# Seven products for the last down pair of groups 0 and 1, in a linear-attention block mixed with a gated feed-forward

## The chip, the cores and the metric

The kernel runs on one core of one Trainium2 chip. The metric is the device time of one execution in microseconds; the time before is the median of three runs.

## What is computed

```python
B, S, D = 1, 2048, 640;  F = 1536;  H = 32; Dh = 20
g = sigmoid((x * gate_w).sum(-1, keepdims=True))
# a: linear attention
q, k, v = split heads of x @ wqkv
phi = lambda t: where(t > 0, t + 1, exp(t)) + 1e-6
pq, pk = phi(q), phi(k)
kv = einsum("bhsd,bhse->bhde", pk, v);  z = pk summed over s
o = einsum("bhqd,bhde->bhqe", pq, kv) / (einsum("bhqd,bhd->bhq", pq, z) + 1e-6)
a = o @ wo
# b: gated feed-forward
b = (sigmoid(x @ w_gate) * (x @ w_up)) @ w_down
out = g * a + (1 - g) * b          # all float32
```

## The kernel before

**Layout.** Everything is transposed: rows of 128 features on the partitions, tokens along the free axis. The 2048 tokens are four groups of 512 (`TG`), D is 5 chunks of 128 (`KC`), F is 12 blocks of 128 (`FC`). A float32 product is three matmuls in a reduced format: each operand is split in a high half (a ScalarE copy that rounds) and a low half (a VectorE subtraction), and `mm3` (lines 406 to 408) multiplies high by high, high by low, low by high. Below, a "product" is one `mm3` of 128 x 128 weights by 128 x 512 values, and a "form" is an operand with its two halves.

**Seven products for eight.** Where two groups and two chunks make a 2 x 2 by 2 x 2 block product, the kernel uses the seven products of Winograd's form of Strassen's method, on sums of the operands (S1 to S4 of the weights, T1 to T4 of the values). Partial results are shared by seeding a PSUM bank with another bank's contents (a ScalarE copy) and adding further products to it.

**Stages.** The keys' side comes first and yields a 640 x 640 matrix M. Then `f_phase` runs the feed-forward for two groups at a time: groups 2 and 3 first (`pr` = 1), then groups 0 and 1 (`pr` = 0). For each of the 12 f blocks, `Block.s1` to `s7` compute gate and up for both groups; gate ends in the tiles c11 (group 0) and c12 (group 1), which become h. After every two f blocks `down_pair` multiplies h by that pair's rows of `w_down` and adds the ten results (5 chunks o, 2 groups g) to the tile `tb`. It is a generator: `f_phase` runs its four parts between steps 3, 4, 5 and 7 of the odd f block that follows. Inside it `new` starts a product in a fresh bank, `go` adds one to a bank, `seed` copies a bank, `out` adds a bank to `tb` on VectorE. B11, B21 are h of the pair's two f blocks for the first group, B12, B22 for the second; T1 = B11 - B12, T2 = B22 - T1, T4 = B21 - T2, T3 = B22 - B12.

The last pair (f blocks 10 and 11) has no following f block. `tail_f` makes plain forms of its h, and `last_down` computes its ten results in two products each (`down_term`, `down_unit`), 20 products. For `pr` = 0 three of the ten banks are seeded with `tb` and copied back by ScalarE, the others are added to `tb` on VectorE.

Last comes the attention part: p (phi of q, kept in DRAM as `p_dram`) is loaded, scaled by factors (`pq_scale`, VectorE), split into `pq`, and multiplied by M: first groups 2 and 3 by `a_unit` (each five terms of `mm3`, one for each chunk of M), then groups 0 and 1 by `ABlock`, which adds its results to `tb`.

**The order of the work.** The instruction order of every engine is written out when the kernel is built. The class `Order` keeps model clocks for TensorE, ScalarE and VectorE. Work that isn't tied to a place is queued with its costs; `order.fill()` puts in what ends no later than the model's TensorE clock plus a slack (`slack_a`, `slack_v`; `order.slack(False)` is 0.6 and 1.2 us). The queues have ranks: `items`, `lazy`, `chain`, `spare`; `streams` are taken by due time, some 2 us ahead (`EARLY`) at the latest. `order.need(key)` emits all that is queued under the key there and then. DMAs are issued by SyncE (`sp`) and GpSimd (`gp`), each in program order.

Of the kernel before, what the change touches and what calls it, by code (L numbers as in the profile page):

```python
# [373 lines left out]
def gated_mix_kernel(ctx: ExitStack, tc: tile.TileContext, xt, xn, wk, wv, wo, wst_q, wst_f, out_t):  # L374
# [1285 lines left out]
    def queue_m(u=0):  # L1660

        raw = down_pool[1].tile([P, D], F32, name="mr", tag="mr")
        m_rows(raw, None, sp, u)

        def fn():
            t = down_pool[1].tile([P, 2, D], F32R, name="mt", tag="mt")
            split(t[:, 0], t[:, 1], raw)

            def rest():
                gp.dma_start(mp_dram[:, u], f32(t))  # L1670
                if u + 1 < KC:
                    queue_m(u + 1)
            order.then(rest)
        order.add(a_cost(D), v_cost(D), fn, "m", lambda: order.when(raw) + 2, spare=True)

    def m_close():
# [106 lines left out]
    def tail_s(f, blk):  # L1783
# [37 lines left out]
    seen = set()  # L1821

    def down_pair(pr, p):
# [4 lines left out]
        def weights(form, q):  # L1828
            c = at[form] + 2 * q * P if form in at else (2 * D - P, D - P)[form == "w1"]
            if not pr:  # L1830
                h, l = (wf[0][:, i] for i in range(2))
            elif c < 2 * D:
                (h, l), c = WD["f", 1, 2 * p + 1 - c // D], c % D
            else:
                (h, l), c = DS[p], c - 2 * D
            return h[:, c:c + P], l[:, c:c + P]
# [21 lines left out]

        if pr:
            for j in range(2):  # L1860
                order.need(("d", ("f", 1, 2 * p + j)))
# [54 lines left out]

    def down_unit(pr, f, o, g, ps=None, seeded=False):
# [6 lines left out]
        if seeded:  # L1924
            act(dst, ps, AF.Copy, "p")
        else:
            add(dst, ps, dst, "p")

# [79 lines left out]
    def f_phase(pr, q, hooks={}):  # L2008
# [7 lines left out]
        for f, s in [(0, 1), (0, 2)] + [e for f in range(FC) for e in f_steps(f)]:  # L2016
            order.plan[pr, f, s] = at
            at += mm * n_mm[s]
        order.plan[pr, FC + 1, "d0"] = at - EARLY

        def step(f, s):
# [24 lines left out]
            if s == 7:  # L2046
                tails[f] = tail_f(f, blk, f == FC - 2) if f >= FC - 2 else tail_s(f, blk)
            if f + 2 < FC and not pr:
# [27 lines left out]
        for f in range(FC):  # L2076
# [53 lines left out]
    def last_down(pr, units):  # L2130
# [3 lines left out]
        order.slack_a, order.slack_v = 0.6, 0.8  # L2134
        if pr:
            omg = f32(down_pool[1].tile([P, 2, 8 * P], F32R, name="ds", tag="ds"))[:, :, :TG]
# [7 lines left out]

        seeds = {} if pr else {5: "cc", 7: "ch", 9: "cc"}

        def seed(i):
            if i in seeds:
                g, o = divmod(i, KC)
                early[i] = ps_tile(seeds[i])  # L2150
                act(early[i], tb[:, o, g], AF.Copy)
        for i in units[:4]:
            g, o = divmod(i, KC)
            if i not in seeds:
                early[i] = ps_tile("rot" if (o + g) % 2 else "dd")
            down_term(early[i], pr, FC - 2, o, g, i not in seeds)
        for i in units:
            g, o = divmod(i, KC)
            if i in seeds and i > 3:
                down_term(early[i], pr, FC - 2, o, g, False)  # L2160
            down_unit(pr, FC - 2, o, g, early.pop(i, None), i in seeds)
            seed(i + 4)
            if pr:
                order.add(0, v_cost(TG), lambda i=i: scaled(i), ("tb", i),
                          lambda: order.vec + 0.6, lazy=True)
            order.fill()
# [74 lines left out]
    def load_p(g):  # L2241

        n = groups.index(g)
        if n == 0:
            PL[g] = [tt("pl") for _ in range(KC - 1)]
            PL[g].append(f32(wu_tile()).rearrange("p a b -> p (a b)")[:, :TG])
            for u in range(KC):
                sp.dma_start(PL[g][u], p_dram[:, u, g])
        else:
            PL[g], PL[g, "t"] = [], []  # L2250
            for u in range(0, KC, 2):
                t = (x2_tile if n == 1 else h_tile)(dt=F32)
                w = min(2, KC - u)
                sp.dma_start(t[:, :w], p_dram[:, u:u + w, g])
                PL[g] += [t[:, i] for i in range(w)]
                PL[g, "t"].append(t)
        PL[g, "at"] = lambda: max(order.when(t) for t in PL[g])

    def load_b(g):
# [3 lines left out]
        elif g == groups[0]:  # L2263
            BL[g] = [ct("bl") for _ in range(KC)]
            for o in reversed(range(KC)):
                sp.dma_start(BL[g][o], b_dram[:, o, g - 2])
# [36 lines left out]
    def queue_pq(g):  # L2303
        for u in range(KC):
            order.add(a_cost(TG), v_cost(TG), lambda u=u: split(*PQ[g][u], PL[g][u]), ("pq", g, u))

# [51 lines left out]
    def queue_pt():  # L2358
# [22 lines left out]
        return queue  # L2381

    def a_first():
# [222 lines left out]
```

## Time and profile before

| | |
|---|---|
| runs | 730.27, 730.38, 730.37 us; median 730.37 |
| profiled execution | span 728.6 us from the first to the last instruction; the page gives no other time for it, and the median is 1.77 us above the span |
| TensorE (PE) | busy 724.0 us (99%), 3569 matmuls |
| VectorE (DVE) | busy 564.0 us (77%) |
| ScalarE (ACT) | busy 360.1 us (49%) |
| GpSimd (POOL) | busy 97.0 us (13%) |
| DMA | 173.54 MB, mean 238 GB/s |
| granted TensorE clock | 1.000 |

In the rows that follow, a line such as `L423 DVE TENSOR_TENSOR tb<-dd,tb` names the source line (423, a helper), the engine, the operation and the tiles, output first; `x3` is the number of instructions merged into the row. Times are microseconds from the start of the span unless they are the nanoseconds of one instruction. The busy time of TensorE counts overlapping matmuls once; the spacing of their starts is what one costs.

### The profile page before, as it was taken

Reading aid. Unit: us, or ns where it says so; the run is one execution under the profiler, and the core shown is the slowest. Engines: PE = TensorE matmul, PEld = TensorE weight load, DVE = VectorE, ACT = ScalarE, POOL = GpSimd, SP = SyncE. Lnnn points to the kernel's source line nnn. Section 1 sums busy time; section 2 is a strip of 40 time slices with the busy share of each in tenths; the row PEclk is TensorE's granted clock in tenths of the full one; section 3 lists DMA queues with packets and bytes.
Section 4 is the critical chain, followed back from the end, with each engine's and each line's share of the span. In section 5 each row is a group of like instructions: output and inputs, shape, how many; then the busy total and the mean of one; then the engine's idle time right before and its main releaser. Section 6 shows DMA issues by size and latency. Waiting matters only on the chain.

```text
span 728.6 us, 10106 instructions
## 1 busy us (share of the span) xinstructions
PE 724.0 (99%) x3569; PEld 622.6 (85%) x3569; DVE 564.0 (77%) x989; ACT 360.1 (49%) x668; POOL 97.0 (13%) x161
## 2 busy tenths in 40 slices
PE   9999999999999999999999999999999999999997
PEld 8999999988888888888888888888888888888886
DVE  6899778987687889888999973547685867698783
ACT  6884649357657653545355363354332332334550
POOL 0211111113212211211110031001000041000000
PEclk9999999999999999999999999999999999999999
DMA  8565658698787866557687288879889697869212
GB/s 269 148 181 111 183 129 253 146 343 292 266 315 260 331 220 232 199 223 252 260 327 261 98 300 321 304 233 339 266 285 325 219 330 210 292 221 337 85 61 102
DMA packets 72841, 173.54 MB, mean 238 GB/s; under 512 B 11690, under 2 KB 35258, under 8 KB 69206
## 3 DMA queue, kind: packets, MB, share of 16 engines
q1 hardware_dynamic: 55526, 109.99, 46.4%
q0 software_dynamic: 17120, 62.74, 24.4%
q8 instruction: 28, 0.46, 0.2%
q14 instruction: 23, 0.19, 0.1%
q10 hardware_dynamic: 144, 0.16, 0.1%
HBM read 103.96 MB, written 63.92 MB: 230 GB/s over the span
## 4 chain that ended last, share of the span: by engine, by line
PE 99%; DVE 0%; issue 0%
PE ch L406 11%; PE ch L407 11%; PE ch L408 11%; PE cc L407 9%; PE cc L408 9%; PE cc L406 9%; PE dd L407 8%; PE dd L408 8%; PE dd L406 8%; PE rot L407 6%; PE rot L408 6%; PE rot L406 6%; PE rot L1505 1%; PE rot L494 0%; PE ch L980 0%; PE dd L980 0%
## 5 line engine op out<-in xcount | busy, mean ns | idle before, releaser
L419 ACT ACTIVATE c<-ch 128x512 f32<-128x512 f32 x52 | 31.1, 598 | 94.9 <-PE ch L408 94.9
L423 DVE TENSOR_TENSOR hf<-c,hf 128x512 fp32r<-128x512 f32 x75 | 51.1, 687 | 24.7 <-ACT hf L419 24.4
L419 ACT ACTIVATE hf<-c 128x512 fp32r<-128x512 f32 x75 | 46.0, 625 | 27.3 <-DVE c L423 27.2
L423 DVE TENSOR_TENSOR c<-cc,c 128x512 f32<-128x512 f32 x40 | 27.6, 690 | 37.5 <-PE cc L408 23.8
L406 PE MATMUL ch<-xth,ws 128*128 128x512 f32 x112 | 43.7, 390 | 0.0
L408 PE MATMUL ch<-xth,ws 128*128 128x512 f32 x112 | 43.6, 389 | 0.0
L407 PE MATMUL ch<-xtl,ws 128*128 128x512 f32 x112 | 43.6, 389 | 0.0
L423 DVE TENSOR_TENSOR tb<-rot,tb 128x512 f32<-128x512 f32 (+1 forms) x61 | 39.3, 674 | 3.0 <-PE rot L408 3.0
L423 DVE TENSOR_TENSOR tb<-dd,tb 128x512 f32<-128x512 f32 x44 | 30.2, 686 | 8.7 <-PE dd L408 8.7
L406 PE MATMUL dd<-xrh,wg 128*128 128x512 f32 x90 | 35.2, 391 | 0.0
L408 PE MATMUL dd<-xrh,wg 128*128 128x512 f32 x90 | 35.1, 389 | 0.0
L407 PE MATMUL dd<-xrl,wg 128*128 128x512 f32 x90 | 35.0, 389 | 0.0
L419 ACT ACTIVATE c<-dd 128x512 f32<-128x512 f32 x22 | 13.1, 597 | 43.6 <-PE dd L408 43.6
L423 DVE TENSOR_TENSOR c<-c,c 128x512 f32<-128x512 f32 x46 | 31.6, 687 | 2.6 <-ACT c L419 2.0
L406 PE MATMUL cc<-xbh,ws 128*128 128x512 f32 x84 | 32.7, 389 | 0.0
L407 PE MATMUL cc<-xbl,ws 128*128 128x512 f32 x84 | 32.7, 389 | 0.0
L408 PE MATMUL cc<-xbh,ws 128*128 128x512 f32 x84 | 32.7, 389 | 0.0
L419 ACT ACTIVATE dd<-ch 128x512 f32<-128x512 f32 x22 | 12.8, 582 | 33.6 <-PE ch L408 33.6
L423 DVE TENSOR_TENSOR wst<-wst 128x256 f32<-128x256 f32 (+2 forms) x69 | 27.4, 413 | 1.4
L408 PEld LDWEIGHTS ch<-xth,ws 128*128 128x128 f32 x112 | 21.0, 188 | 4.7 <-DVE ws L423 0.3
L407 PEld LDWEIGHTS ch<-xtl,ws 128*128 128x128 f32 x112 | 21.0, 188 | 4.3
L406 PEld LDWEIGHTS ch<-xth,ws 128*128 128x128 f32 x112 | 21.0, 188 | 4.2
(643 smaller groups left out, 2354.1 us busy)
## 6 DMA issues: line engine op xcount, KB each, us to landing
wf<-ws POOLq DMA_DIRECT2D x12, 1152.0 KB, 7.5
ws<-wf SPq DMA_DIRECT2D x11, 1152.0 KB, 8.2
wst<-wst_f SPq DMA_DIRECT2D x12, 640.0 KB, 5.0
wf<-wg POOLq DMA_DIRECT2D x12, 640.0 KB, 6.5
wd<-wd POOLq DMA_DIRECT2D x12, 640.0 KB, 7.9
wg<-wf SPq DMA_DIRECT2D x12, 640.0 KB, 5.5
wf<-wd SPq DMA_DIRECT2D x10, 640.0 KB, 9.4
xnst<-xn SPq DMA_DIRECT2D x16, 320.0 KB, 3.7
```

What stands on the lines that cost most here:

```text
L406: nc.tensor.matmul(out, l_hi, r_hi, start=first, stop=False, skip_group_check=True)
L407: nc.tensor.matmul(out, l_hi, r_lo, start=False, stop=False, skip_group_check=True)
L408: nc.tensor.matmul(out, l_lo, r_hi, start=False, stop=last, skip_group_check=True)
L419: nc.scalar.activation(out, src, fn, **kw)
L423: nc.vector.tensor_tensor(out, a, b, op=op)
L1505: nc.tensor.matmul(ps[:w, :w], v[:, m, :w], gt[:, m, c0:c0 + w], start=(m == 0), stop=(m == KC - 1))
```

## The change

For groups 0 and 1 the last pair (f blocks 10 and 11) also runs through `down_pair`, in a branch of its own with another order of the products; `last_down` is left to groups 2 and 3. `tail_last` makes its forms. The sums of the weights for that pair are computed by a new chain of spare work (`queue_last_s`, behind the five steps of `queue_m`), stored, and loaded again by `load_last_s`. Four results (`FAR`) are copied out of PSUM by ScalarE and added to `tb` by a transfer that accumulates (`far`), two in the pair of blocks 8 and 9 and two in the last one. The first group's p is loaded in three steps (`load_p0`), its scalings are queued with each load, and its splits are queued after step 5 of block 11 instead of after step 7. `load_ms(1)`, and the scalings and splits of the second group, are queued behind the last pair; group 2's b results are loaded from the first to the last.

```diff
@@ queue_m: after the last of its five steps
+                else:
+                    queue_last_s()
@@
+    def queue_last_s():
+        p, w = FC // 2 - 1, 4 * P
+        raw = [down_pool[1].tile([P, D], F32, name=n, tag=n)[:, :w] for n in ("mr", "mv")]
+        for j in range(2):
+            sp.dma_start(raw[j], wst_f[2 * p + j, :, 2, :w])
...
+        def sums(part):
+            if part == 0:
+                add(a22, a21, a22)
+                sub(a21, a11, a21)
+            else:
+                sub(a11, a22, a11)
+                sub(a12, a12, a11)
+        def form(j):
+            t = down_pool[1].tile([P, 2, D], F32R, name="mt", tag="mt")[:, :, :w]
+            split(t[:, 0], t[:, 1], raw[j])
...
+                gp.dma_start(dst, f32(t))
...
@@ 
+    def tail_last(f, blk):
+        p = f // 2
+        def t3():
+            HR[p, "B21"] = blk.c11
+            h_form(p, "B21")
+        def t4():
+            act(blk.c12, blk.c12, AF.Sigmoid)
+            vec2(blk.c12, blk.c22, blk.c12, OP.mult, "a")
+        def t5():
+            HR[p, "B22"] = HR[p, "T3"] = b22 = blk.c12
+            HR[p, "T2"], HR[p, "T4"], b12 = t2, t4, _ = [HR.pop((p, n)) for n in ("T1", "B21", "B12")]
+            order.need(("h", p, "T1"), False)
+            sub(t2, b22, t2)
+            sub(t4, t4, t2)
+            h_form(p, "B22")
+            h_form(p, "T2")
+            sub(b22, b22, b12)
+        return {3: t3, 4: t4, 5: t5}
...
+    FAR = [(FC // 2 - 2, 1, 0), (FC // 2 - 2, 3, 0), (FC // 2 - 1, 4, 0), (FC // 2 - 1, 0, 0)]
@@ down_pair
+        def far(key, o, g):
+            if not far_at:
+                far_at.extend(down_pool[1].tile([P, D], F32, name="far", tag=n) for n in ("mr", "mv"))
+            t = far_at.pop(0)[:, :TG]
+            act(t, ps[key], AF.Copy, "p")
+            gp.dma_start(tb[:, o, g], t, accum_op=OP.add)
+            order.fill()
...
+            if not pr and (p, o, g) in FAR:
+                far(key, o, g)
+                return
...
+        if p == FC // 2 - 1:
+            new("W", "dd", "w0", "B11")
+            new("X0", "ch", "A11", "B11")
+            seed("V", "dd", "W")
+            new("X1", "ch", "A11", "B11", 1)
+            seed("Y0", "rot", "X0")
+            seed("Y1", "rot", "X1")
+            yield
+            new("Z0", "cc", "S1", "T1")
+            out("Z0", 1, 1)
+            new("Z1", "cc", "S1", "T1", 1)
+            out("Z1", 3, 1)
+            go("V", "w1", "B21")
+            out("V", 4, 0)
+            go("Y0", "A12", "B21")
+            out("Y0", 0, 0)
+            go("Y1", "A12", "B21", q=1)
+            out("Y1", 2, 0)
+            go("W", "w0", "T1")
+            go("X0", "S2", "T2")
+            out("X0", 0, 1)
+            go("X1", "S2", "T2", q=1)
+            out("X1", 2, 1)
+            go("Z0", "S4", "B22")
+            out("Z0", 0, 1)
+            go("Z1", "S4", "B22", q=1)
+            out("Z1", 2, 1)
+            go("X0", "S3", "T3")
+            out("X0", 1, 1)
+            go("X1", "S3", "T3", q=1)
+            out("X1", 3, 1)
+            go("W", "w1", "B22")
+            out("W", 4, 1)
+            go("X0", "A22", "T4")
+            out("X0", 1, 0)
+            go("X1", "A22", "T4", q=1)
+            out("X1", 3, 0)
+            return
@@ f_phase
-        order.plan[pr, FC + 1, "d0"] = at - EARLY
+        if pr:
+            order.plan[pr, FC + 1, "d0"] = at - EARLY
+        else:
+            for s, n in (("d1", 1), (3, 8), ("d2", 13), ("d3", 15)):
+                order.plan[pr, FC + 1, s] = at + mm * n
...
-                    load_ms(1)
...
             else:
+                if not pr:
+                    queue_t1(f // 2)
                 step(f, 6)
...
+            elif not pr:
+                tail_last(f, blocks[f])[3]()
+                order.slack_a, order.slack_v = 0.3, 0.3
             step(f, 7)
@@ 
+    def load_p0(u0, u1):
+        g = groups[0]
+        t = PL.setdefault(g, [])
+        for u in range(u0, u1):
+            t.append(tt("pl") if u < KC - 1 else f32(wu_tile()).rearrange("p a b -> p (a b)")[:, :TG])
+            sp.dma_start(t[u], p_dram[:, u, g])
+            order.add(0, v_cost(TG), lambda u=u: pq_scale(g, u), ("sc", g), lambda u=u: order.when(t[u]) + 1, lazy=True)
...
+    def load_last_s():
+        p = FC // 2 - 1
+        DS[p] = [x2_tile("ds", F32R).rearrange("p a b -> p (a b)") for _ in range(2)]
+        for c in range(2):
+            sp.dma_start(f32(DS[p][c]), wd_dram[p][:, c, 2 * D:])
     tail = f_phase(0, q, {
         (2, 7): [queue_m],
         (FC - 2, 2): [lambda: load_wd(FC - 2)],
-        (FC - 2, 7): [lambda: load_p(groups[0]), lambda: queue_scale(groups[0], True)],
-        (FC - 1, 2): [lambda: load_wd(FC - 1)],
+        (FC - 3, 4): [lambda: load_p0(0, 2)],
+        (FC - 2, 3): [lambda: load_p0(2, 4)],
+        (FC - 2, 7): [lambda: load_p0(4, 5)],
+        (FC - 1, 2): [lambda: load_wd(FC - 1), load_last_s],
+        (FC - 1, 5): [a_first],
         (FC - 1, 7): [lambda: load_m(1)],
     })
-    for s in (3, 4, 5):
-        tail[s]()
-    a_first()
+    down = down_pair(0, FC // 2 - 1)
+    order.slack_a = order.slack_v = -9.0
+    tail[4]()
+    next(down)
+    tail[5]()
+    order.slack_a, order.slack_v = 0.6, 0.8
+    for name in ("T3", "T4"):
+        queue_h(FC // 2 - 1, name)
     load_p(groups[1])
-    pq_tiles(groups[1])
     for g in groups[:2]:
         load_b(g)
+    for _ in down:
+        pass
+    order.slack(False)
+    load_ms(1)
+    pq_tiles(groups[1])
     queue_scale(groups[1])
     queue_pq(groups[1])
-    last_down(0, range(2 * KC))
```

More of the change, by code (lines that the diff above doesn't have):

```diff
@@ L1672, in rest @@
                     queue_m(u + 1)
+                else:
+                    queue_last_s()
             order.then(rest)
         order.add(a_cost(D), v_cost(D), fn, "m", lambda: order.when(raw) + 2, spare=True)
+    def queue_last_s():
[3 more added lines that the diff above has]
+            sp.dma_start(raw[j], wst_f[2 * p + j, :, 2, :w])
+        (a11, a21), (a12, a22) = [r.rearrange("p (q h c) -> h p q c", q=2, h=2) for r in raw]
+        at = lambda: max(order.when(r) for r in raw) + 1
+        ready = [at]
+        def sums(part):
[8 more added lines that the diff above has]
+            split(t[:, 0], t[:, 1], raw[j])
+            dst = wd_dram[p][:, :, 2 * D + j * w:2 * D + (j + 1) * w]
+            ready[0] = lambda: 1e9
+            def rest():
+                gp.dma_start(dst, f32(t))
+                ready[0] = lambda: order.when(dst)
+            order.then(rest)
+        for part in range(2):
+            order.add(0, 2 * v_cost(2 * P), lambda part=part: sums(part), "m", at, spare=True)
+        for j in range(2):
+            order.add(a_cost(w), v_cost(w), lambda j=j: form(j), "m", lambda: ready[0](), spare=True)
     def m_close():
@@ L1915, in down_term, with down_unit @@
         mm3(ps, h[:, os_], l[:, os_], *HT[f, g], first, not first)
[L1917 removed]
+    def down_unit(pr, f, o, g, ps=None):
         if ps is None:
@@ L1923, in down_unit @@
         dst = tb[:, o, g]
[L1924 to L1927, printed above, removed]
+        add(dst, ps, dst, "p")
     def q_phase(pr, b12, extra):
@@ L2046, in step @@
             if s == 7:
-                tails[f] = tail_f(f, blk, f == FC - 2) if f >= FC - 2 else tail_s(f, blk)
+                tails[f] = tail_f(f, blk, f == FC - 2) if pr and f >= FC - 2 else tail_s(f, blk) if f < FC - 1 else tail_last(f, blk)
             if f + 2 < FC and not pr:
@@ L2143, in scaled @@
             gp.dma_start(b_dram[:, o, g], tb[:, o, g])
[L2145 to L2151, printed above, removed]
         for i in units[:4]:
             g, o = divmod(i, KC)
-            if i not in seeds:
-                early[i] = ps_tile("rot" if (o + g) % 2 else "dd")
-            down_term(early[i], pr, FC - 2, o, g, i not in seeds)
+            early[i] = ps_tile("rot" if (o + g) % 2 else "dd")
+            down_term(early[i], pr, FC - 2, o, g, True)
         for i in units:
             g, o = divmod(i, KC)
[L2159 to L2165, printed above, removed]
+            down_unit(pr, FC - 2, o, g, early.pop(i, None))
+            order.add(0, v_cost(TG), lambda i=i: scaled(i), ("tb", i),
+                      lambda: order.vec + 0.6, lazy=True)
             order.fill()
@@ L2241, in load_p @@
     def load_p(g):
[L2243 to L2256, printed above, removed]
+        PL[g], PL[g, "t"] = [], []
+        for u in range(0, KC, 2):
+            t = (x2_tile if g == groups[1] else h_tile)(dt=F32)
+            w = min(2, KC - u)
+            sp.dma_start(t[:, :w], p_dram[:, u:u + w, g])
+            PL[g] += [t[:, i] for i in range(w)]
+            PL[g, "t"].append(t)
         PL[g, "at"] = lambda: max(order.when(t) for t in PL[g])
@@ L2264, in load_b @@
             BL[g] = [ct("bl") for _ in range(KC)]
-            for o in reversed(range(KC)):
+            for o in range(KC):
                 sp.dma_start(BL[g][o], b_dram[:, o, g - 2])
@@ L2304, in queue_pq @@
         for u in range(KC):
-            order.add(a_cost(TG), v_cost(TG), lambda u=u: split(*PQ[g][u], PL[g][u]), ("pq", g, u))
+            order.add(a_cost(TG), v_cost(TG), lambda u=u: split(*PQ[g][u], PL[g][u]), ("pq", g, u), lambda: PL[g, "at"]())
     def scale_b(g, o):
@@ L2381, in queue_pt @@
         return queue
+    def load_p0(u0, u1):
[5 more added lines that the diff above has]
+            order.add(0, v_cost(TG), lambda u=u: pq_scale(g, u), ("sc", g), lambda u=u: order.when(t[u]) + 1, lazy=True)
+        PL[g, "at"] = lambda: max(order.when(t) for t in PL[g])
     def a_first():
```

8 lines of the change are left out of this document (4 added, 4 removed).

## The prediction

> **What bounds the kernel now.** I read the page first, then the busy time by windows for the stage that changes, then the timelines of TensorE, VectorE and ScalarE there. The first two lines below are the page's busy time, the next its chain of work that ended last.
>
> ```profile
> span 728.6 us, 10106 instructions
> PE 724.0 (99%) x3569; PEld 622.6 (85%) x3569; DVE 564.0 (77%) x989; ACT 360.1 (49%) x668; POOL 97.0 (13%) x161
> PE 99%; DVE 0%; issue 0%
> ```
>
> TensorE is the bound, and its own order of matmuls is the chain: nothing else ends last anywhere. So a matmul that goes is worth its full spacing, and every wait that the change puts ahead of a matmul is paid in full. The stage that changes, by windows (columns: PE, PEld, DVE, ACT, POOL, each busy us and instructions, then clock, DMA share, GB/s) and by the timeline of TensorE (start, us, engine, ...):
>
> ```profile
> 645.65:659.25 13.60, 13.60 (x62) 11.27 (x60) 11.62 (x19) 6.62 (x12) 0.00 (x0) 1.00 0.99 374
> 634.77:645.65 10.88, 10.88 (x50) 9.01 (x48) 10.18 (x18) 1.75 (x3) 0.00 (x0) 1.00 0.12 31
> 645.42 0.39 PE L408 MATMUL cc<-xbh,ws 128*128 128x512 f32 x1
> 645.65 0.39 PE L406 MATMUL dd<-hf,wg 128*128 128x512 f32 x1
> 659.02 0.39 PE L408 MATMUL cc<-hf,wg 128*128 128x512 f32 x1
> 659.25 0.39 PE L406 MATMUL rot<-pq,ws 128*128 128x512 f32 x1
> ```
>
> The second window is the end of f block 11 (second half of step 5 to step 7), the first is `last_down`: 60 weight loads, so 60 matmuls, in 13.60 us, 0.2267 us each, 0.680 us for a product of three. The clock is granted in full. From 659.25 the attention part runs (`a_unit`). VectorE is busy 10.18 of 10.88 us in the second window while TensorE never waits: it is almost full, and can become the bound.
>
> **The change: products.** `last_down` has 2 blocks x 5 outputs x 2 groups = 20 products. The new branch of `down_pair` has 5 `new` and 13 `go`, 18 products. Removed: 2 x 3 matmuls x 0.2267 = 1.36 us. All of it is on the path, since PE is 99% of the chain. By the Trainium skill (TensorE: Matmul & The Clock Gate, Back-to-back issue gap) a 512-column matmul that is warm follows the last after N / 2.4 + 2.5 ns, 216 ns, which would make it 1.29 us. I take the row.
>
> **The chain behind step 7.** The old order ran four independent products first; the new one needs sums of the last block's result. What the chain costs, from the rows of before (the step's last matmul is the 645.42 row above):
>
> ```profile
> 645.85 0.69 DVE L423 TENSOR_TENSOR c<-cc,c 128x512 f32<-128x512 f32 x1
> 646.57 0.63 ACT L419 ACTIVATE c<-c 128x512 f32<-128x512 f32 x1 [3.62 <-DVE c L423]
> 647.24 0.69 DVE L423 TENSOR_TENSOR c<-c,c 128x512 f32<-128x512 f32 x1
> 648.03 0.63 ACT L419 ACTIVATE hf<-c 128x512 fp32r<-128x512 f32 x1 [0.82 <-DVE c L423]
> 615.71 1.41 DVE L423 TENSOR_TENSOR c<-c,c 128x512 f32<-128x512 f32 x2
> 653.25 1.89 DVE L423 TENSOR_TENSOR pq<-pl,pq 128x512 fp32r<-128x512 f32 x3
> 649.60 1.66 ACT L419 ACTIVATE pq<-pl 128x512 fp32r<-128x512 f32 x3
> ```
>
> A VectorE pass is 0.69 us, one that waits for the pass before it starts 0.72 after it (1.41 for two), independent ones follow every 0.60 (1.89 for three); ScalarE's copies follow every 0.52. A result can be read 0.43 us after its last matmul starts, 0.88 after its product starts. Let t = 0 be the start of the first down product behind step 7 (645.65 in the old trace).
>
> - Add 0.20, sigmoid 0.92, product with c22 1.59, T2 = B22 - T1 at 2.31, T4 = B21 - T2 at 3.03 (both wait for the one before).
> - ScalarE after the sigmoid: three PSUM seeds (V, Y0, Y1; 1.44, 1.96, 2.48), then the high halves of B22 (3.00) and T2 (3.52).
> - VectorE: low half of B22 3.66, of T2 4.26 (done 4.95), T3 4.86.
> - TensorE meanwhile: W, X0, X1 on B11 from 0; Z0, Z1 on T1 from 2.04; V, Y0, Y1 on B21 from 3.40; W on T1 5.44; X0 and X1 on T2 from 6.12. So T2 is a microsecond early; no wait.
>
> **Results added on VectorE.** 14 results are taken out of PSUM in the last pair; two of them (V, Y0) go by ScalarE and a transfer, 12 stay on VectorE. From 5.46, every 0.60: Z0 5.46, Z1 6.06, Y1 6.66, low half of T3 7.26 (the planner starts it some 2 us ahead of its due time, 13 products), X0 7.86, X1 8.46, low half of T4 9.06, Z0 9.66, Z1 10.26, X0 (output 1, group 1) 10.86, done 11.55. The seventeenth product, X0 on T4, adds to the same PSUM bank, which must have been read; without a wait it would start at 16 x 0.680 = 10.88. It starts near 11.58. **Wait: 0.70 us.** X1's bank is read by 12.15, its product starts at 12.26: nothing more. If VectorE is one pass behind at t = 0, the wait is 1.3; if the chain is two passes quicker than my list, nothing. I take 0.70, since every start in the list is a spacing from a row.
>
> **The sum.** 728.6 - 1.36 + 0.70 = 727.94 of span. The page gives no time of the profiled execution other than its span; the median of the runs, 730.37, is 1.77 above it, and no part of the change lies outside the span. 727.94 + 1.77 = 729.7.
>
> **Steps at nothing, and their cover.** The p work of before and the steps that move (the first three rows from VectorE's timeline; the others from the tiles `mr` and `mt`, with first and last start):
>
> ```profile
> 634.22 0.68 DVE L427 SCALAR_TENSOR_TENSOR pl<-pl,fac 128x512 f32<-128x512 f32 x1
> 645.19 0.68 DVE L427 SCALAR_TENSOR_TENSOR wu<-wu,fac 128x512 f32<-128x512 f32 x1
> 656.57 0.69 DVE L423 TENSOR_TENSOR pq<-wu,pq 128x512 fp32r<-128x512 f32 x1
> L363 POOL DMA_DIRECT2D mr<-m_dram x4: 574/576/583, 594.2 to 598.1; - x4
> L419 ACT ACTIVATE mt<-mr x5: 723/740/742, 487.5 to 535.2; 128x640 fp32r<-128x640 f32 x5
> L363 POOL DMA_DIRECT2D mt<-m_dram x8: 574/574/612, 586.7 to 593.1; - x8
> L423 DVE TENSOR_TENSOR mv<-mr,mv x1: 425/425/425, 701.4 to 701.4; 128x256 f32<-128x256 f32 x1
> ```
>
> - First p: five scalings (634.22 to 645.19) and five splits (653.25 to 656.57) lay beside f block 11 and `last_down`. Now SP issues two loads after step 4 of block 9, two after step 3 of block 10 and one at the old place, its step 7; by the products that the code puts in between (31 in block 11, 18 in block 10, 27 left of block 9) at t = -52, -32 and -21. Behind them on SP queue factor and gate loads of groups 0 and 1 and weights, none of which is needed at once. The scalings follow the loads, and the splits are asked for from step 5 of block 11, t = -10.88. VectorE had 18 passes in that window. New: 5 scalings and one late half go, two results go to ScalarE, and T1's difference, its low half, B21's low half and 5 split halves come: 18 again. It fits with nothing to spare; with up to three splits left over, they run while the first `a_unit` works through its five terms (0.68 each against 0.60): nothing. All five left over cost 1.5.
> - Four results by transfers: ScalarE copies, POOL issues an accumulating transfer. The copies of V (4.3) and Y0 wait for the tiles `mr`, `mv`, which the transfers of pair 4 free; behind them in ScalarE stand the high halves of T3 and T4. Their landing:
>
> ```profile
> zacc<-kr POOLq DMA_DIRECT2D x8, 320.0 KB, 4.2
> wd<-wd POOLq DMA_DIRECT2D x12, 640.0 KB, 7.9
> ```
>
>   Accumulating transfers of 320 KB landed in 4.2 us, the slowest POOL stores in 7.9. Issued near t = -2.0, they may take 8.7 us before T3 (needed at 8.84) is late. Nothing.
> - Weight sums for pair 5 (`queue_last_s`): two loads, four 256-wide and two 512-wide VectorE passes, two ScalarE copies, two POOL stores, behind the fifth `mt` at 535.2. Five such steps took 47.7 us, 11.9 each; two more end near 561, before the forced end at block 9 (586.7). Nothing; forced, VectorE would wait for a load, up to 8 us.
> - `load_ms(1)`: eight POOL loads move from 594 to behind the last pair; they are first used at 701.4, now 43 us after their issue. The loads of the pair's sums (SP, ahead of block 11's 31 products) have 21 us. SP then issues the b loads, whose tiles are free by 5.6.
>
> **The rivals.**
>
> 1. No wait (0.20): 728.6 - 1.36 + 1.77 = 729.0. For it: the second window shows VectorE at 18 passes in 10.88 us without a TensorE gap. Against: here the chain of five dependent passes leaves VectorE standing for 1.1 us (four passes take 3.46 instead of 2.4). It is 0.19% faster; a tail shorter by 0.1 us would carry it over 0.2%, about what a measurement of this kernel can tell from no change. I give that 0.07 of the 0.20.
> 2. A longer wait (0.12): VectorE a pass behind at t = 0 and all five splits left: 0.7 + 0.6 + 1.5 = 2.8; 730.37 - 1.36 + 2.8 = 731.8. Just within 0.2%.
> 3. **Slower: first p not ready (0.15).** If VectorE has no room in blocks 10 and 11, scalings and splits are left for the wait ahead of the first `a_unit` (t = 12.9), behind the last two results (13.9). With n scalings left, the first split's low half is done at 13.9 + 0.6 n + 0.7, wanted at 13.1: 1.5 + 0.6 n. With n = 2: net -1.36 + 0.70 + 2.7 = +2.0, 732.4; n = 5: +3.8, 734.2. It decides from n = 2 on. For it: 10.18 busy of 10.88. Against: four of the five loads go out 31 and 11 us sooner than before.
> 4. Slower: transfers hold ScalarE (0.05). Landing of 13 us instead of 4.2 makes T3 late by 4.3: 734.0. Decides at 11.5 us; no POOL row is that long.
> 5. Slower: a long wait also slows TensorE (0.04). The first matmuls of the program run at half pace:
>
> ```profile
> 0.85 3.57 PE rot L494 x8
> ```
>
>    0.446 us each, against 0.2267. If a wait of 4 us brings that back for eight matmuls, 1.75 us come on top of rival 3: about 736. The Trainium skill says so (TensorE: Matmul & The Clock Gate, Why this matters for your kernels: "No PE-idle gaps >~3µs between matmul bursts"); no gap of that length stands in this trace behind the start, so no row shows it for the middle of a kernel.
>
> **How the numbers follow.** The forecast, a wait of 0.70 (0.3 to 1.4), has 0.44: 729.7, 729.3 to 730.4. Faster by over 0.2% (under 728.9): 0.07. Within: 0.13 of rival 1, 0.44, rival 2's 0.12: 0.69. Slower (over 731.8): 0.15 + 0.05 + 0.04 = 0.24. The range 728.9 to 732.5 takes in all of the forecast and rivals 1 and 2 and the start of rival 3; about 0.2 is left out.
>
> **What would show it.** 6 matmuls fewer; 54 between step 7's last and the first `a_unit`, 12.24 us without a wait, 12.9 by my list, with one wait, for a VectorE pass on `tb<-ch`, ahead of the last two products. T2 early; no ScalarE idle ahead of a `far` copy over 1 us; all scalings of p before the last pair. Wrong: a TensorE wait of over 3 us at the first `pq` matmul (rival 3), ScalarE waiting for a transfer (rival 4), or waits elsewhere, from blocks 3 to 9, which would say that the moved loads or the weight sums were not free.

## The result, and the profile after

The changed kernel takes 741.48 us (median of five runs, 739.89 to 742.20) where the kernel before takes 730.27 (five runs beside them, 729.76 to 730.38). The ratio is 1.0149, interval 1.0137 to 1.0162: 1.5% slower, 11 us, and outside the predicted range, which ended at 732.5. The profiled execution took 741.73 us, with a span of 740.0.

The page of after: its span and busy time, the slices of the granted clock, and the chain that ended last.

```profile
span 740.0 us, 10154 instructions
PE 728.2 (98%) x3563; PEld 624.1 (84%) x3563; DVE 572.9 (77%) x1005; ACT 363.8 (49%) x674; POOL 101.9 (14%) x167
PEclk9999999999999999999999999999999999989999
PE 10%; DVE 0%; issue 0%
```

Six matmuls went, as the change says (3569 to 3563), and yet PE is busy 4.2 us longer: some matmuls take longer than they did, and one slice of the clock row shows an 8. The chain is no help here: it names 10% of the span instead of 99%. The waits of PE say where to look (us in total, times, longest):

```profile
PE ch L406 <- DVE tb L423: 4.0, 1, 4.0
PE dd L406 <- DVE tb L423: 2.6, 1, 2.6
PE rot L494 <- PEq L2717: 0.8, 1, 0.8
PE rot L407 <- DVE pq L423: 0.5, 1, 0.5
```

The third stands in before too (0.8 us, the first matmul of the program) and was its only one. The other three are new. Both long waits are said to be for VectorE, but VectorE is only the messenger, as the timelines show.

**The wait at 563.** The timeline of after (start, us, engine, operation, in brackets the idle time before and its releaser), cut to the work on the tile `mt` and the matmul that waited:

```profile
553.39 0.68 POOL L363 DMA_DIRECT2D wd<-mt  x1 [13.07 <-DVE mt L423]
...
557.27 0.59 ACT L419 ACTIVATE cc<-rot 128x512 f32<-128x512 f32 x1
...
563.92 0.63 ACT L419 ACTIVATE mt<-mv 128x512 fp32r<-128x512 f32 x1 [6.07 <-issue]
564.58 0.69 DVE L423 TENSOR_TENSOR mt<-mv,mt 128x512 fp32r<-128x512 f32 x1 [6.19 <-ACT mt L419]
...
565.93 0.50 PE L406 MATMUL dd<-hf,wf 128*128 128x512 f32 x1 [2.57 <-DVE tb L423]
```

and the last line of the answer for the tile `mt` (545 to 580 us):

```profile
DMA to landing us min/median/max: 2.3/2.7/10.5
```

`queue_last_s` makes two forms in one buffer, the tile `mt`. The first is stored from 553.39; that store is the longest, 10.5 us, and ends at 563.9. The second form's high half is a ScalarE copy into the same buffer, so it cannot start before. ScalarE takes its instructions in the order of the program: from 557.86 on it stands for 6.07 us at this copy, and the next one (`c<-ch`) follows at 564.46. VectorE, whose next instruction in order is the low half of the same form, stands for 6.19 us, and its next results for `tb` come after that. TensorE runs on for some microseconds with the banks that it has, and then waits from 562.97 to 565.93: 2.96 us instead of a spacing of 0.23. "issue" in the third row is what the profile says when it has no releaser to show; the landing of the store gives it.

**The wait at 659.** The end of the last pair. t = 0 is the first down product, at 650.86. ScalarE, VectorE and TensorE, each in its own order:

```profile
659.15 0.60 ACT L419 ACTIVATE far<-dd 128x512 f32<-128x512 f32 x1 [4.22 <-DMA tb<-far]
661.27 0.60 ACT L419 ACTIVATE far<-rot 128x512 f32<-128x512 f32 x1 [1.51 <-DMA tb<-far]
661.76 1.14 ACT L419 ACTIVATE hf<-c 128x512 fp32r<-128x512 f32 x2
```

```profile
651.06 0.69 DVE L423 TENSOR_TENSOR c<-cc,c 128x512 f32<-128x512 f32 x1
652.45 2.14 DVE L423 TENSOR_TENSOR c<-c,c 128x512 f32<-128x512 f32 x3 [0.70 <-ACT c L419]
656.32 1.28 DVE L423 TENSOR_TENSOR tb<-cc,tb 128x512 f32<-128x512 f32 x2
657.51 0.68 DVE L423 TENSOR_TENSOR tb<-rot,tb 128x512 f32<-128x512 f32 x1
662.41 0.69 DVE L423 TENSOR_TENSOR hf<-c,hf 128x512 fp32r<-128x512 f32 x1 [4.22 <-ACT hf L419]
```

```profile
659.47 0.39 PE L408 MATMUL cc<-hf,ds 128*128 128x512 f32 x1
663.85 0.77 PE L406 MATMUL ch<-hf,ds 128*128 128x512 f32 x1 [3.99 <-DVE tb L423]
...
668.25 0.63 PE L407 MATMUL ch<-hf,wg 128*128 128x512 f32 x1
...
671.25 0.49 PE L407 MATMUL rot<-pq,ws 128*128 128x512 f32 x1 [0.45 <-DVE pq L423]
```

The tile `far` (`mr`, `mv`), from the answer for that name: the transfers' issues, what ScalarE waited for, and the time from issue to landing.

```profile
L363 POOL DMA_DIRECT2D tb<-far x4: 839/863/1090, 648.6 to 662.2; - x4
  DMA tb<-far: 5.7, 2
DMA to landing us min/median/max: 6.7/9.0/11.9
```

Two results of pair 4 leave from 648.56 and 649.24 and land after 10.5 and 11.9 us, at 659.07 and 661.18. Only then are their tiles free for the copies of V and Y0, which start at 659.15 and 661.27; and behind these two copies, in ScalarE's order, stand the high halves of T3 and T4. The low half of T3, forecast for t = 7.26, starts at 662.41 (t = 11.55); behind it in VectorE's order are the results X0 and X1. TensorE starts X0 on T3 at 663.85 instead of 659.70.

**The granted clock after the waits.** By windows (PE, PEld, DVE, ACT, POOL, each busy us and instructions; then clock, DMA share, GB/s):

```profile
563.00:566.00 3.00, 0.43 (x3) 0.07 (x1) 1.42 (x3) 1.11 (x2) 0.43 (x1) 1.00 0.95 362
566.00:570.00 4.00, 4.00 (x10) 2.64 (x11) 4.00 (x7) 0.00 (x0) 0.38 (x2) 0.57 0.40 153
659.50:664.00 4.50, 0.51 (x3) 0.18 (x2) 1.59 (x3) 2.98 (x7) 1.68 (x2) 0.78 1.05 372
664.00:669.00 5.00, 5.00 (x12) 3.95 (x13) 4.08 (x7) 0.46 (x1) 1.67 (x3) 0.51 1.10 296
```

In and behind each long wait the clock is granted at half, by the trace's clock records from 566.47 to 569.88 and from 662.04 (before the second wait has ended) to 668.87. In the last window 12 matmuls take 5.00 us, with a full PE and no wait. That is why PE is busier with fewer matmuls.

**The account.** From the starts of the matmuls, each against a spacing of 0.2267 us:

| | us |
|---|---|
| six matmuls fewer | -1.36 |
| the wait at 563, and the slow matmuls and a short wait (0.4) to 570 | 2.73 + 1.87 = +4.60 |
| the wait at 659 and the slow matmuls to 669 | 4.15 + 2.44 = +6.59 |
| the wait for a split of p at 670.4 | +0.73 |
| the first 7 us of the program, where the change has no work (the clock is in full from 6.69 us, in the kernel before from 5.92) | +0.5 |
| sum | +11.1 |
| the two spans, 740.0 - 728.6 | +11.4 |

### The profile page after: what moved, and what is told of

It reads as the page before. It is cut to its first block, busy times and chain, and to the rows that moved or that the text cites. A ratio compares the mean times of both kernels' runs of the same rounds, so it can differ in the third digit from the quotient of the medians.

```text
span 740.0 us, 10154 instructions
## 1 busy us (share of the span) xinstructions
PE 728.2 (98%) x3563; PEld 624.1 (84%) x3563; DVE 572.9 (77%) x1005; ACT 363.8 (49%) x674; POOL 101.9 (14%) x167
## 5 line engine op out<-in xcount | busy, mean ns | idle before, releaser
L423 DVE TENSOR_TENSOR hf<-c,hf 128x512 fp32r<-128x512 f32 x78 | 53.0, 686 | 25.9 <-ACT hf L419 25.6
L419 ACT ACTIVATE hf<-c 128x512 fp32r<-128x512 f32 x78 | 47.7, 624 | 24.9 <-DVE c L423 24.9
L423 DVE TENSOR_TENSOR tb<-rot,tb 128x512 f32<-128x512 f32 (+1 forms) x58 | 37.4, 673 | 3.0 <-PE rot L408 3.0
L423 DVE TENSOR_TENSOR c<-c,c 128x512 f32<-128x512 f32 x50 | 34.3, 686 | 3.3 <-ACT c L419 2.7
L423 DVE TENSOR_TENSOR tb<-dd,tb 128x512 f32<-128x512 f32 x40 | 27.4, 685 | 7.8 <-PE dd L408 7.8
```

What stands on the lines that cost most here:

```text
L419: nc.scalar.activation(out, src, fn, **kw)
L423: nc.vector.tensor_tensor(out, a, b, op=op)
```

## The experiments

The theory: two transfers that land later than 10 us hold a tile that ScalarE must write again, its queue stops, and TensorE pays the wait and then a stretch at half pace. It has two places that can be undone separately. Rivals: VectorE itself is too full (then taking the transfers' waits away doesn't help), and the accumulation makes the transfers slow (then plain stores land early).

**1 and 2. One cause each.** The first lets the planner place the second form of `queue_last_s` 8 us of its model's time later, and nothing else:

```diff
-                ready[0] = lambda: order.when(dst)
+                ready[0] = lambda: order.when(dst) + 8
```

> The second form of the stored weight sums is queued 8 us later (in the planner's time), everything else is as in the changed kernel. Theory W (ScalarE stands in its queue for a transfer still in flight, and a wait of some 3 us brings half pace for a few us): the wait at 563 (2.7 us) and the slow matmuls behind it (1.9 us) both go, 741.5 - 4.6 = 736.9 us; the wait at 659 stays. Rival V (VectorE is too full in block 7): the wait stays, over 740. Rival C (the half pace has another cause than the wait): only 2.7 goes, 738.8.

Measured: 736.77 us (735.75 to 736.99), ratio 1.0080 (1.0065 to 1.0095). ScalarE's row for the copy and what is left of PE's long waits:

```profile
562.76 0.64 ACT L419 ACTIVATE mt<-mv 128x512 fp32r<-128x512 f32 x1 [0.72 <-DVE c L423]
```

```profile
PE ch L406 <- DVE tb L423: 4.2, 1, 4.2
```

The copy now stands behind another one in ScalarE's order and starts 0.1 us after the store has landed (562.68), so ScalarE is idle for 0.72 us instead of 6.07; the low half has moved behind six results for `tb` in VectorE's order. The row names VectorE; in experiment 3, with the same edit, the row of this copy names the store (0.49 us). The wait at 563 and its slow matmuls are gone, and 4.7 us with them: the first entry of the account is shown.

The second leaves pair 4's two results on VectorE, so that `mr` and `mv` are free when the last pair asks for them; the early form stays:

```diff
-    FAR = [(FC // 2 - 2, 1, 0), (FC // 2 - 2, 3, 0), (FC // 2 - 1, 4, 0), (FC // 2 - 1, 0, 0)]
+    FAR = [(FC // 2 - 1, 4, 0), (FC // 2 - 1, 0, 0)]
```

> Only the two results of the last pair go by transfer (outputs 4 and 0 of group 0), so that no copy has to wait for an earlier transfer to leave its tile; the two of the pair before are added on VectorE again. Theory W: the wait of 4.15 us at 659 and 2.4 us of slow matmuls go, the list of the prediction is left: a wait of 0.7, and up to 1.5 for splits of p that two more VectorE passes push behind the pair: 741.5 - 6.6 + 0.7 = 735.6 (to 737.1). Rival V (VectorE is the bound there anyway, the transfer only stands in front of it): over 739.

Measured: 734.40 us (733.66 to 735.94), ratio 1.0054 (1.0040 to 1.0068). The wait of 4 us is gone; 1.05 us (X0 on T4) and 0.87 (a split of p) are left, start to start. It came out 1.2 us better than I wrote, and the windows of the first wait, which this kernel keeps, say why:

```profile
562.00:564.20 2.20, 0.43 (x3) 0.02 (x1) 1.37 (x3) 1.12 (x2) 0.38 (x1) 1.00 1.03 388
564.20:567.00 2.80, 2.35 (x8) 1.33 (x9) 2.80 (x5) 0.00 (x0) 0.32 (x1) 1.00 0.75 282
```

Here the store happened to land in 9.7 us instead of 10.5, the gap in TensorE's starts was 2.16 us instead of 2.96, and the clock stayed at 1.00; two waits of 0.4 us for VectorE's results are left behind it. That is this execution, of 733.66 us. Of the other three, the one of 733.91 also has a mean clock of 0.999, and the two of 734.89 and 735.94 have 0.997, about what one stretch of 3.4 us at half clock takes off.

**3. Both.** The two edits together.

> Both edits of the two other runs together. Theory W: 731.0 us (730.3 to 732.5), of which 0.7 is the wait for VectorE and the rest splits of p; no matmul at half pace behind the start. Rival V: over 734.

Measured: 731.35 us (730.59 to 732.75, 11 runs), ratio 1.0014 (1.0005 to 1.0022). Both causes account for all but 1 us of the 11. What is left, by PE's timeline:

```profile
655.97 0.47 PE L406 MATMUL ch<-hf,ds 128*128 128x512 f32 x1 [0.78 <-DVE tb L423]
...
658.97 0.47 PE L406 MATMUL ch<-hf,wg 128*128 128x512 f32 x1 [0.69 <-DVE tb L423]
...
661.96 0.50 PE L407 MATMUL rot<-pq,ws 128*128 128x512 f32 x1 [0.48 <-DVE pq L423]
```

With pair 4's two results back on VectorE, it comes into the last pair 1.35 us late (with t = 0 at 645.94, the add that the forecast's chain begins with is at t = 1.55 instead of 0.20), and X0 waits twice, on T3 and on T4.

**4. Other results, earlier.** Late form, and pair 4 sends Y1 and Y0, which are ready earlier, so that the tiles come free in time:

```diff
+    FAR = [(FC // 2 - 2, 2, 0), (FC // 2 - 2, 0, 0), (FC // 2 - 1, 4, 0), (FC // 2 - 1, 0, 0)]
```

> The later form, and four results by transfer as in the change, but the two of the pair of blocks 8 and 9 are outputs 2 and 0 of group 0, which are ready some 10 us earlier, when SyncE loads nothing. Theory W: these transfers have landed before the tiles are wanted again; landing near the 4 us of the accumulating transfers at the start of the kernel, since little else moves then; 729.7 to 730.5 us. Rival A (an accumulating transfer into this tile takes 10 us by itself): they land in 10 us, still just in time, and the time is the same; only the row of the landing tells the two apart. Rival V: over 734.

Measured: 732.95 us (731.06 to 733.22), ratio 1.0025 (1.0014 to 1.0037). A miss. ScalarE no longer waits for a transfer, but the first two, issued at 633.6 and 634.3, still take 9.1 and 10.3 us. SyncE has issued loads of weights, p and `mp_dram` from 629.0 to 632.3, so the expectation that it loads nothing there was wrong (266 to 338 GB/s from 634 to 640). TensorE has four short waits (starts 0.82, 1.20, 1.08 and 0.87 us apart): VectorE is relieved early, where it had room (busy 0.04 us from 638 to 640), and not later, where it hasn't (busy without a break from 640 to 648).

**5. No transfers at all.** Late form, `FAR = []`.

> The later form, and no result by transfer: all 14 results of the last pair, and all of the pair before, are added on VectorE. By the prediction's list of VectorE passes, with what the run of both edits showed (VectorE 1.1 us behind at the start of the pair): two more passes of 0.60 ahead of X0's first result make that wait 2.0, X0 on T4 another 1.0, the splits of p 0.6: 730.4 - 1.4 + 3.6 = 732.6 us. If the transfers relieved nothing (VectorE is not what the pair waits for), 731.3, as with two of them.

Measured: 735.75 us (734.88 to 738.19), ratio 1.0077 (1.0063 to 1.0092). A miss by 3 us, in the direction of the rival: VectorE alone cannot take the results.

```profile
661.18 0.47 PE L406 MATMUL ch<-hf,ds 128*128 128x512 f32 x1 [2.02 <-DVE tb L423]
```

Beside this wait (2.41 us from start to start, with seven matmuls at 0.43 us behind it) there are waits in the blocks before: 0.98 us at 494, 0.52 at 627, 1.11 at 629. The profiled execution, 738.19, is the longest of the four. The transfers are worth having; it is what they hold that costs.

**6. Without accumulation.** Late form; the four results go to a scratch tensor in DRAM by plain stores instead of being added to `tb`, so four results lack their last part:

```diff
+    far_dram = dram.tile([P, 2, TG], F32, name="far_dram")
...
-            gp.dma_start(tb[:, o, g], t, accum_op=OP.add)
+            gp.dma_start(far_dram[:, len(far_at)], t)
```

> The later form, and the four transfers of the change with the same tiles, but each a plain store to a scratch tensor in DRAM; the four results are left out of the output. Theory A (it is the addition that takes long, reading and writing the tile): the two behind block 11's step 6 land in 4 to 5 us, as stores of 256 KB did, ScalarE does not stand, 730.3 us. Theory Q (the loads that SyncE issues beside them, 2240 KB and more, hold the queues): they land in 9 us or more as before, and the wait of 4 us and the half pace stay, 736 to 737 us.

Measured in a single run: 731.72 us. The landings are 2.9, 8.9, 7.0 and 6.0 us. The groups of DMA issues between 643 and 662 us (KB each, median us from issue to landing):

```profile
bl<-b_dram SPq DMA_DIRECT2D x5, 256.0 KB, 10.3
far_dram<-far POOLq DMA_DIRECT2D x4, 256.0 KB, 6.5
```

So a plain store too takes up to 8.9 us here: the accumulation is a part of the 10 to 12 us (a packet of 2048 bytes takes a DMA engine 176 ns when it accumulates, and 84 to 98 as a plain load), and the company of SyncE's loads is the other. (The plain store also goes to DRAM and not to the tile `tb`, so the two differ in more than the accumulation.) Experiment 12 shows the other half.

**7. Tiles of their own.** Late form; all four transfers as in the change, but the last pair's two copies go into the halves of an h tile that is free by then, and not into `mr` and `mv`:

```diff
-    seen, far_at = set(), []
+    seen, far_at, far_n = set(), [], []
...
-                far_at.extend(down_pool[1].tile([P, D], F32, name="far", tag=n) for n in ("mr", "mv"))
+                if far_n:
+                    h = h_tile(F32)
+                    far_at.extend(h[:, j] for j in range(2))
+                else:
+                    far_at.extend(down_pool[1].tile([P, D], F32, name="far", tag=n) for n in ("mr", "mv"))
+                far_n.append(1)
```

> The later form, and the four transfers of the change, the two of the last pair from a tile of their own (the two halves of an h tile that is free), so that no copy waits for a landing. Theory W: the wait at 659 goes whole, the two transfers ahead of the pair let VectorE start it on time: the prediction's 0.70, and 0.6 for the splits of p: 730.4 - 1.36 + 1.3 = 730.3 us. Rival (the transfers' traffic itself, or their issue, costs time elsewhere): 731.3 or more.

Measured: 730.69 us (730.22 to 731.25, 11 runs), ratio 1.0004 (0.9995 to 1.0012): level with the kernel before. The first two transfers still take as long as in the change, and cost nothing, because nothing waits for their tiles. The DMA issues and, in the second fence, what is left of PE's waits:

```profile
bl<-b_dram SPq DMA_DIRECT2D x5, 256.0 KB, 17.8
...
tb<-far POOLq DMA_DIRECT2D x2, 256.0 KB, 11.2
tb<-hf POOLq DMA_DIRECT2D x2, 256.0 KB, 8.4
```

```profile
657.24 0.47 PE L406 MATMUL ch<-hf,wg 128*128 128x512 f32 x1 [0.61 <-DVE tb L423]
...
660.24 0.50 PE L407 MATMUL rot<-pq,ws 128*128 128x512 f32 x1 [0.48 <-DVE pq L423]
```

The first is X0 on T4, the seventeenth product, 0.77 us late; the second is a split of p, 0.64. Together, 1.41 us, they take back the 1.36 that the six matmuls gave.

**8. Six results by transfer.** Experiment 7, with (5, 2, 0) and (5, 4, 1) by ScalarE and a transfer as well, to take the last 0.77 off VectorE.

> As the run with own tiles, and two more results of the last pair by transfer (output 2 of group 0, output 4 of group 1; four halves of two h tiles). By the list X0 on T4 then waits 0.1 instead of 0.7, and the splits of p come 0.6 to 1.2 sooner and wait no more: 730.4 - 1.36 + 0.1 = 729.2 us (to 729.7), faster than before. If ScalarE or the transfers become the bound, 730.3 or more.

Measured: 736.72 us (735.05 to 739.43), ratio 1.0088 (1.0073 to 1.0102). A miss by 7 us. Inside the pair it did what I wrote: one short wait (starts 0.57 us apart) and none for a split. But the transfers crowd the loads behind them:

```profile
670.74 0.60 ACT L419 ACTIVATE ch<-bl 128x512 f32<-128x512 f32 x1 [12.08 <-DMA bl<-b_dram]
```

The b results, which `a_unit` seeds its banks with, land at 667 to 671 us instead of 657 to 662 in the kernel before. In experiment 7, with four transfers, they land at 667 to 669, and no long wait stands there, so it is the last 2 us that cost. TensorE's starts are 3.19 us apart there, with half pace behind it, and 2.7 us more of waits stand between 707 and 719.

**9, 10, 11. The b loads ahead of the p loads.** In SyncE's order, group 2's b before group 3's p (`groups` is 2, 3, 0, 1):

```diff
+    load_b(groups[0])
...
-    for g in groups[:2]:
-        load_b(g)
+    load_b(groups[1])
```

with six results by transfer, with five (without (5, 4, 1)), and with the four of experiment 7:

> As the run with six transfers, but group 2's b is loaded ahead of group 3's p. There the wait of 3 us in the attention part came from b landing some 10 us later than before the change, since the accumulating transfers hold the DMA queues longer than plain ones. With 1280 KB less ahead of it b lands 3 to 5 us sooner, that wait goes: 730.4 - 1.36 + 0.4 = 729.4 us, if the waits behind 700 (2.7 us) came from it too; 732 if they stay. Rival (the transfers, not the order of the loads, set b's landing): 735 or more as before.

> As the run with own tiles, one more result by transfer (output 2 of group 0), and b loaded ahead of p. One VectorE pass less: X0 on T4 waits 0.2 instead of 0.77, the splits of p wait 0.3 instead of 0.7: 730.4 - 1.36 + 0.5 = 729.5 us if b lands in time; 732 or more if not.

> As the run with own tiles (730.7 us, waits 1.6), b loaded ahead of p, nothing else. If the loads are no longer what the pair waits for, the same waits and 730.5 to 730.7 us.

Measured, in this order: 732.64 us (732.37 to 733.60), ratio 1.0036 (1.0022 to 1.0050); 733.17 us (732.64 to 733.97), 1.0041 (1.0028 to 1.0053); 730.58 us (730.20 to 731.84, 11 runs), 1.0004 (0.9995 to 1.0013). With six, the wait of 3.19 us is gone, as expected, and the pair's starts are again 0.57 us apart; but the waits behind 700 stay. With five, the pair's starts are 0.65 us apart and 2.7 us of waits stand behind 700. The waits of VectorE in experiment 9:

```profile
DVE cc L423 <- DMA omg<-gate_dram: 4.1, 1, 4.1
DVE pl L427 <- DMA pl<-p_dram: 3.9, 3, 2.8
```

VectorE loses some 7 us there, is then full (busy 9.79 of the 10 us from 700, where before has 8.94), and TensorE waits 3.26 us in all. That the loads of p and of the factor `omg` are later is in the rows; whether they alone make it, or the planner's new order too, was not tried and is open. Experiment 11 shows that the order of the loads is worth nothing by itself.

**12. The transfers in another place.** Late form, and only two results by transfer, those of pair 3, 40 us earlier: `FAR = [(FC // 2 - 3, 1, 0), (FC // 2 - 3, 3, 0)]`.

> The later form, and only two results by accumulating transfer, those of outputs 1 and 3 of group 0 in the pair of blocks 6 and 7, beside block 9's last steps, where SyncE loads a third of what it loads behind block 11. The landing by itself: 4 to 6 us if what made the others 9 to 12 is the loads beside them; 9 or more if an accumulating transfer takes that long alone. The last pair adds all on VectorE, so the time is near the run without transfers, 735 us.

Measured in a single run: 734.63 us, since VectorE has all results of the last two pairs to itself (TensorE's starts 2.39, 1.08 and 0.87 us apart at the end). The answer for the tile:

```profile
DMA to landing us min/median/max: 3.7/4.5/5.3
```

The same accumulating transfers of 256 KB land in 3.7 and 5.3 us here and in 10.5 and 11.9 at 649. So it is not the accumulation by itself: it is the accumulation beside a stretch of large loads.

No version beat the kernel before. The nearest, experiments 7 and 11, are level with it.

## Why the prediction was wrong

**Right: the products.** 3563 matmuls, six fewer, at 0.2267 us each.

**Right: the chain behind step 7.** With t = 0 at 650.86, the add is at 0.20 (forecast 0.20), the product with c22 at 1.59 (1.59), Z0 at 5.46 (5.46), Y1 at 6.65 (6.66). From the low half of T3 on, the list no longer holds in the changed kernel, because of the transfers. In experiment 7, which has the change without their waits, the list holds to its end: the low half of T3 starts at 7.26 (7.26), X0 at 7.85 (7.86), and X0 on T4 at 11.68 (11.58), a wait of 0.77 us, forecast 0.70. The wait of the seventeenth product is thus shown as the kernel's own limit, that of VectorE.

**Wrong: "Four results by transfers ... Nothing".** This is the step that failed, with 6.59 us. The mechanism stood in the text: the copies of V and Y0 wait for `mr` and `mv`, the halves of T3 and T4 stand behind them, and a landing of up to 8.7 us is free. The size was wrong. I took the landing from the rows of the queue as they stood in before, 4.2 and 7.9 us, medians of transfers at other times, and let the slowest median stand for a bound. Single landings in before were longer: up to 9.3 us for the accumulating transfers, and for the tile `mt`, whose transfers are all GpSimd's,

```profile
DMA to landing us min/median/max: 4.6/8.0/12.5
```

The stretch of the last pair has SyncE's loads of `mp_dram`, p and b beside it, and the transfers took 10.5 and 11.9. Rival 4 was this case and had a chance of 0.05 ("no POOL row is that long"), which holds for the medians and not for the longest. Its own working would have given the wait well enough: 11.9 is 3.2 later than 8.7, with the 0.70 of the forecast 3.9, measured 4.15. Its time, 734.0, lacked the half pace.

**Wrong: "Weight sums for pair 5 ... Nothing".** 4.60 us. I counted the step's work, as if its time were all that it could cost, and saw a danger only in its forced end. It isn't forced; it comes early. The planner put the second form into ScalarE's order by its model's time of the store, about 6 us before the store had landed. The prediction's text lists "two POOL stores" and one `mt` buffer is in the diff; that the second form must wait for the first store was there to be read. Both failures are among the signs of being wrong that the prediction named: ScalarE waiting for a transfer, and a wait in blocks 3 to 9.

**Rival 5's half pace.** It gave this to rival 3, a wait at the first `pq` matmul, which did not come; half pace came all the same, behind the other two waits. The gaps in TensorE's starts and what followed them:

| gap, us | kernel | spacing of the matmuls behind it, us | time at half clock, us |
|---|---|---|---|
| 2.16 | experiment 2, at 562 | 0.23, with two waits of 0.4 | 0 |
| 2.39 | experiment 12, at 656 | 0.23 | 0 |
| 2.41 | experiment 5, at 659 | 0.43 for 7 | 3.41 |
| 2.96 | after, at 563 | 0.43 for 5 | 3.41 |
| 3.19 | experiment 8, at 668 | 0.43 for 5 | 3.41 |
| 4.38 | after, at 659 | 0.43 for 10 | 6.83 |
| 4.56 | experiment 1, at 654 | 0.43 for 11 | 6.83 |

The row for the last, by windows:

```profile
658.80:664.30 5.50, 5.50 (x13) 4.34 (x14) 4.24 (x8) 0.60 (x2) 1.89 (x4) 0.51 1.09 299
```

The rule cited in the prediction (the Trainium skill, TensorE: Matmul & The Clock Gate, Why this matters for your kernels: no PE-idle gaps over about 3 us) holds for the three gaps above 3 us. But half pace came behind 2.96 and 2.41 us too, so in these kernels the limit lies lower.

The length of a gap alone does not decide it either: 2.39 us passed and 2.41 did not. The clock records of the traces show more. Every stretch at half clock lasts 3.41 us or twice that, and all changes of the clock in one trace lie whole multiples of 3.41 us apart, as if the clock were set anew at each step. Experiment 5's gap, 658.77 to 661.18, lies within one such step, and half clock begins with the next:

```profile
658.41:661.82 3.41, 1.39 (x7) 0.88 (x6) 3.41 (x7) 1.25 (x3) 0.00 (x0) 1.00 1.03 362
661.82:665.23 3.41, 3.41 (x10) 2.63 (x9) 3.19 (x6) 0.00 (x0) 0.00 (x0) 0.50 1.04 390
```

Experiment 12's gap, 655.71 to 658.10, has a border of these steps inside it (657.21), with 1.50 us on one side and 0.89 on the other. Over the seven gaps, half clock followed where at least 2.41 us of a gap lay in one step, and did not where at most 1.83 did (experiment 2). That this decides is inferred from these gaps; no run moved a gap against the steps.

**Splits of p: nothing.** Small miss: a split is late in nearly every version, by 0.6 to 0.7 us. The prediction allowed "up to three splits left over" for nothing; in experiment 7 they cost 0.64, which, with the 0.77, gives back all that the products won.

**Rivals 1, 2 and 3** did not come: there is no version without a wait, and the last scaling of the first p starts at 643.21 in the changed kernel, ahead of the last pair, so that at the first `pq` product only the 0.6 us for a split are waited.

## What to carry to other kernels

A buffer that a transfer still reads stops more than its next writer: everything behind that writer in the order of its engine stops too, so ask of every copy into a reused tile what stands behind it. Take the landing time of a transfer from rows that have the same traffic beside them, and its longest, not its median; the same 256 KB took 3.7 us in one stage and 11.9 in another. A wait of TensorE near 3 us is not paid once: in the changed kernel the matmuls behind the two waits, at half pace, lost another 0.6 to 0.7 times as much.

## What the runs showed of the hardware

- A packet of an accumulating transfer occupies a DMA engine about twice as long as one of a plain load: 176 ns (median) for 2048 bytes, against 84 to 98 ns (`after`, 650 to 664 us, and experiment 7).
- Accumulating transfers and loads hold each other up: the transfers landed in 3.7 to 5.3 us at 606 and in 10.5 to 11.9 at 649, and b landed 9 to 10 us later than in the kernel before with six of them (experiment 8), 7 to 9 with four (experiment 7). The b loads took 17.8 us (median) beside four of them and 10.3 beside plain stores (experiment 6); those whose landing the traces have were issued within 0.5 us of each other in the two kernels.
- The step from a harmless wait to half pace lies within 1 us of wait. A landing 0.8 us shorter (experiment 2) was worth 0.8 us of wait and 0.7 of what follows: 1.9 us were lost behind the wait in the changed kernel, and 1.2 in experiment 2, at full clock, to VectorE's results.
- Half pace makes a part of the scatter. Of the changed kernel's five runs, that of 739.89 us has a mean clock of 0.995 and the four of 740.72 to 742.20 have 0.993: one stretch of 3.41 us at half clock is 0.0023 of 740. It is not the only cause: experiment 3 scatters by 2.2 us with 0.999 or more in every run.
